# Moving one 64-column subtraction from VectorE to GpSimd in the start-up of a fused attention and MLP kernel

## The chip, the cores and the metric

One core of a Trainium2 chip. The metric is the time of one execution in device microseconds (us). Each run on record has a state, fast or slow, judged from its time and its granted TensorE clock; all runs told of here are fast, with a clock of 0.998 to 1.000.

## The reference

Clustered attention, 4 batches, 8 heads, 768 positions, 64 dimensions: q, k and the 16 centroids of a head are normalised, each q and k row is assigned to the nearest centroid, and attention runs only between rows of equal assignment. The result (3072 x 512) goes through an MLP with exact GELU.

```python
q_assign = np.argmax(np.einsum('bhsd,hcd->bhsc', q_n, c_n), axis=-1)
k_assign = np.argmax(np.einsum('bhsd,hcd->bhsc', k_n, c_n), axis=-1)
mask = q_assign[:, :, :, None] == k_assign[:, :, None, :]
scores = np.where(mask, scale * np.matmul(q, k.transpose(0, 1, 3, 2)), -1000000000.0)
# softmax over the last axis, times v; then gelu(x @ w_in) @ w_out
```

## The kernel before

The kernel computes in fp16. Where fp16 is too coarse for an argmax, a value is kept as two halves: a high part (the cast to fp16) and a low part (the value less the high part). This is done for q and k of every head and once for the centroids, before the first head. A table gives the order of all operations; each engine runs its own in that order (VectorE's in the profile of the kernel before begin so: `cn` 4.85 us, `lok0` 5.27, `chi` 5.75, `clo` 6.00, `loq0` 6.74), and a name with an engine behind it (`hiq0@POOL`) is put there. POOL is GpSimd, DVE is VectorE, ACT is ScalarE, PE is TensorE. The table's part that matters:

```python
TABLE = (
    "loadq0 zero3 ident cent dm ones ssq zero2 root hiq0@POOL loadk0 hik0 eps rnorm "
    "loadk2 loadk1 cn lok0 exptab chi hik1 warm256 ... warm128 trk0 loadq1 clo ctr "
    "cc loq0 trq0 hiq1 loadk3 loadv5 evk0 warm256 ... asnk0 evq0@DVE warm256 ... asnq0 "
    "lok1 hik2 ... trk1 lok2 ... loq1@DVE trq1 amax0 ge0 ... ohtr0 ... sc0a2 ...")   # cut
```

`hik0` is the high part of head 0's k and `lok0` its low part, `trk0` the transposes of both on TensorE, `evk0` the copy of the transposes out of PSUM. `chi` and `clo` are the centroids' high and low parts, `ctr` their two transposes, `cc` the copy of these to `c_cat`, `asnk0` the assignment matmuls, `sc0a2` the first scores. `warm` is a filler matmul that nobody reads. The three operations in question:

```python
c6 = add("DVE", 0.17, -75, lambda: nc.vector.tensor_copy(
    cent_hl[:, 0], cent_n.to_broadcast([H * C, 2, D])), [c5], name="chi")
c7 = add("DVE", 0.22, -74, lambda: nc.vector.tensor_sub(
    cent_hl[:, 1, 0], cent_n[:, 0], cent_hl[:, 0, 0]), [c6], name="clo")
...                                                  # cut
def lo(eng, w=w):                                    # lok0, loq0 on DVE; lok1, lok2 on POOL
    t = T[w + "st", i]
    engine[eng].tensor_sub(t[:, :, D:2 * D], T[w + "raw", i], t[:, :, 0:D])
```

The softmax here doesn't subtract the row's maximum and nothing guards it: scores larger than these inputs give would overflow.

## Time and profile before

| | before |
|---|---|
| median of the first 3 runs | 291.01 us (290.45 to 291.35) |
| span in the profile | 289.3 us, TensorE busy 283.1 |
| q's transposes of head 0 begin | 7.34 us |
| first score matmul begins | 11.89 us |

In a line of the timeline the first number is the start, the second the duration (both us), then engine, source line, operation, output<-inputs and shape; the bracket gives the idle time before it and what ended it. In the lines of waits the numbers are the total, the count and the longest. One more view of the kernel before is ScalarE's timeline: the casts of head 0's and head 1's k.

```profile
4.73 0.51 ACT L381 CAST st<-k_raw 128x384 f16<-128x384 f32 x1 [1.78 <-DMA k_raw<-in_k_dram]
5.15 0.20 ACT L427 ACTIVATE tab<-dm 128x1 f32<-128x1 f16 x1
5.25 0.49 ACT L381 CAST st<-k_raw 128x384 f16<-128x384 f32 x1
```

GpSimd's subtraction for head 1 follows the second cast by 0.08 us; VectorE's for head 0 follows the first.

### The profile page before, as it was taken

To read this page: it belongs to the slowest core of one execution; us is meant where nothing else is said; L and a number is where in the kernel's file an instruction comes from. 1 tells how busy PE (TensorE), PEld (TensorE's weight loads), DVE (VectorE), ACT (ScalarE), POOL (GpSimd) and SP (SyncE) were. 2 spreads that over 40 slices of the span, in tenths; PEclk is the share of its full clock that TensorE was granted. 3 is DMA by queue.
4 is the path that set the end of the run, shared out by engine and by line. 5 is a ranking of instruction groups with operands and counts; after the bars stand their busy time and mean duration, and the time that the engine had idled before them with its cause. 6 is when DMAs were issued, how large, how long until landed. Compare 5 with 4: busy or idle time off the path is not lost.

```text
span 289.3 us, 8384 instructions
## 1 busy us (share of the span) xinstructions
PE 283.1 (98%) x3411; PEld 213.3 (74%) x3411; DVE 206.9 (72%) x501; ACT 232.4 (80%) x323; POOL 108.7 (38%) x151
## 2 busy tenths in 40 slices
PE   7999999999999999999999999999999999999995
PEld 5888776677687777766688888765687788766884
DVE  4899777788989765354997656536769953798853
ACT  3899998699999999857799898767899888498410
POOL 6889971306011714313302644106430020429410
PEclk9999999999999999999999999999999999999999
DMA  7899999577947979949458988656241243010123
GB/s 254 256 241 254 251 292 238 120 130 164 240 120 152 222 183 172 198 132 206 114 139 184 196 210 148 130 159 112 56 97 51 54 103 84 0 57 0 39 76 124
DMA packets 78039, 43.11 MB, mean 149 GB/s; under 512 B 55473, under 2 KB 78001, under 8 KB 78001
## 3 DMA queue, kind: packets, MB, share of 16 engines
q1 hardware_dynamic: 73056, 37.76, 56.7%
q0 software_dynamic: 4224, 4.19, 9.0%
q10 hardware_dynamic: 720, 0.62, 0.6%
q8 instruction: 26, 0.43, 0.6%
q14 instruction: 13, 0.10, 0.1%
HBM read 27.30 MB, written 6.29 MB: 116 GB/s over the span
## 4 chain that ended last, share of the span: by engine, by line
PE 59%; DMA 2%; POOL 1%; DVE 0%; issue 0%; DVEq 0%
PE op L1235 20%; PE hp L919 14%; PE sc_ps L784 11%; PE fx_ps L1055 6%; PE x_ps L816 6%; DMA kqT<-st 2%; PE asn_ps L616 1%; POOL st L519 0%; DVE c L1281 0%; POOL c L1295 0%; POOL st L383 0%; PE fin_ps L887 0%; DVEq L1281 0%
## 5 line engine op out<-in xcount | busy, mean ns | idle before, releaser
L793 ACT ACTIVATE p_sb<-sc_ps 128x768 f16<-128x768 f32 x192 | 146.3, 811 | 9.3 <-PE sc_ps L784 6.8
L784 PE MATMUL sc_ps<-kqT 80*128 80x384 f16 x384 | 93.2, 325 | 0.1
L919 PE MATMUL hp<-xt,w_in_sb 128*128 128x384 f16 x384 | 64.8, 326 | 0.0
L816 PEld LDWEIGHTS <-p_sb 128*128 128x128 f16 x1152 | 47.9, 97 | 10.6 <-issue 0.5
L1235 PEld LDWEIGHTS <-g 128*128 128x128 f16 x480 | 45.5, 97 | 12.2
L919 PEld LDWEIGHTS <-w_in_sb 128*128 128x128 f16 x384 | 36.7, 98 | 23.3
L932 ACT ACTIVATE g<-hp 128x768 f16<-128x768 f32 x48 | 38.9, 811 | 16.6 <-PE hp L919 16.0
L816 PE MATMUL x_ps<-vaug,p_sb 128*128 128x65 f16 x1152 | 52.3, 193 | 0.0
L1235 PE MATMUL op<-w_out_sb,g 128*128 128x256 f16 x288 | 40.1, 272 | 0.0
L784 PEld LDWEIGHTS <-kqT 80*128 80x128 f16 x384 | 31.5, 98 | 3.5 <-issue 0.3
L519 POOL TENSOR_TENSOR st<-k_raw,st 128x384 f16<-128x384 f32 x21 | 19.8, 943 | 28.7 <-DVE st L383 15.7
L1235 PE MATMUL op<-w_st,g 128*128 128x256 f16 x192 | 27.0, 272 | 0.0
L519 POOL TENSOR_TENSOR st<-q_raw,st 128x384 f16<-128x384 f32 x20 | 18.5, 923 | 11.7 <-DVE st L383 6.0
L1235 PEld LDWEIGHTS <-S 128*128 128x128 f16 x192 | 18.1, 97 | 5.2 <-issue 0.3
L632 DVE TENSOR_REDUCE asb<-asn_ps 128x192 f32<-128x384 f32 x24 | 13.3, 553 | 9.3 <-PE asn_ps L616 9.2
L843 DVE TENSOR_TENSOR x_tok<-x_ps,rec 128x384 f16<-128x384 f32 (+1 forms) x40 | 19.0, 476 | 1.1
L383 POOL CAST st<-k_raw 128x384 f16<-128x384 f32 x17 | 9.2, 546 | 25.7 <-DMA kqT<-st 16.4
L836 DVE RECIPROCAL rec<-x_ps 128x6 f32<-128x6 f32 (+1 forms) x40 | 7.5, 187 | 15.5 <-PE x_ps L816 14.8
L383 POOL CAST st<-q_raw 128x384 f16<-128x384 f32 x19 | 10.1, 532 | 15.7 <-DMA q_raw<-in_q_dram 10.0
L383 POOL CAST vaug<-v_raw 128x384 f16<-128x384 f32 x17 | 8.6, 511 | 17.1 <-DMA v_raw<-in_v_dram 11.1
L383 DVE COPY p<-op 128x256 f32<-128x256 f32 x19 | 8.0, 422 | 9.0 <-PE op L1235 8.8
L1235 PE MATMUL op<-w_out_sb,S 128*128 128x256 f16 x96 | 13.8, 272 | 0.1
(120 smaller groups left out, 412.5 us busy)
## 6 DMA issues: line engine op xcount, KB each, us to landing
q_raw<-in_q_dram SPq DMA_DIRECT2D x32, 192.0 KB, 4.1
v_raw<-in_v_dram SPq DMA_DIRECT2D x32, 192.0 KB, 3.9
k_raw<-in_k_dram SPq DMA_DIRECT2D x31, 192.0 KB, 4.0
out_dram<-c SPq DMA_DIRECT2D x45, 128.0 KB, 2.5
w_in_sb<-in_moe_w_in_dram POOLq DMA_DIRECT2D x4, 512.0 KB, 8.5
w_out_sb<-in_moe_w_out_dram POOLq DMA_DIRECT2D x4, 512.0 KB, 10.1
out_dram<-c ACTq DMA_DIRECT2D x3, 128.0 KB, 1.8
kqT<-st SPq DMA_TRANSPOSE x22, 4.0
```

What stands on the lines that cost most here:

```text
L383: engine[eng].tensor_copy(o, i)
L519: engine[eng].tensor_sub(t[:, :, D:2 * D], T[w + "raw", i], t[:, :, 0:D])
L632: nc.vector.tensor_reduce(out=T["asb", i], in_=T["asn", i].rearrange("p n w (a c) -> p n w c a", a=2), axis=AX.X, op=ALU.add)
L784: nc.tensor.matmul(s_ps[:, e, 0:QB], T["kT", i][0:D + C, c * 128:(c + 1) * 128], T["qT", i][0:D + C, t * QB:(t + 1) * QB], start=True, sto ...
L793: nc.scalar.activation(T["p", i, t][:, 2 * cp:2 * cp + 2, :], T["sc", i, t, cp][:, :, 0:QB], ACT_FN.Exp, bias=0.0, scale=float(scale))
L816: nc.tensor.matmul(o, T["p", i, t][:, ch, jj * 128:(jj + 1) * 128], vaugs[turn("va", i)][:, ch, 0:D + 1], start=(ch == 0), stop=(ch == N - 1))
L836: nc.vector.reciprocal(T["rec", key], T["x", key][:, :, D:D + 1])
L843: nc.vector.tensor_tensor(T["xtok", b][:, h // 2, j0:j0 + nn, h % 2 * D:(h % 2 + 1) * D], T["x", key][:, :, 0:D], T["rec", key].to_broadca ...
L919: nc.tensor.matmul(T["hp", hb, fp][:, e, 0:QB], w_in_sb[:, m, f * 128:(f + 1) * 128], T["xt", b][:, m, t * QB:(t + 1) * QB], start=(m == 0 ...
L932: nc.scalar.activation(T["g", hb][:, :, fp, :], T["hp", hb, fp][:, :, 0:QB], ACT_FN.Gelu, bias=0.0, scale=1.0)
L1055: nc.tensor.matmul(o, a[p](m), r[p](m), start=start and m == 0, stop=m == 1, skip_group_check=not start)
L1235: nc.tensor.matmul(T["op", b, key], a()[:, f, j * 128:(j + 1) * 128], w[:, f, :], start=(start and f == 0), stop=(f == NB - 1), skip_group ...
```

## The change

The low part of the centroids goes to GpSimd, in front of GpSimd's subtraction for head 1's k. Its intent is to free VectorE for head 0's q, and to have the low part ready earlier. Besides the table's line breaks the diff is:

```diff
-    "... trk0 loadq1 clo ctr "
+    "... trk0 loadq1 clo@POOL "
+    "ctr ..."
-    c7 = add("DVE", 0.22, -74, lambda: nc.vector.tensor_sub(
-        cent_hl[:, 1, 0], cent_n[:, 0], cent_hl[:, 0, 0]), [c6], name="clo")
+    c7 = add("DVE", 0.22, -74, lambda eng: engine[eng].tensor_sub(
+        cent_hl[:, 1, 0], cent_n[:, 0], cent_hl[:, 0, 0]), [c6], alt={"POOL": 0.3}, name="clo")
```

## The prediction

> **What bounds the kernel now.** I read the shares by engine first, then the stretches of time, then who waited for whom on TensorE, then the instructions of the first 13 us in order of time. The page gives the frame:
>
> ```profile
> span 289.3 us, 8384 instructions
> PE 283.1 (98%) x3411; PEld 213.3 (74%) x3411; DVE 206.9 (72%) x501; ACT 232.4 (80%) x323; POOL 108.7 (38%) x151
> ```
>
> TensorE has work for 283.1 of 289.3 us, so at most 6.2 us are idle on it. A change to one 64-element VectorE instruction can only matter where that idle time lies. The busy time by stretches (columns: stretch, its length, then busy us of PE, PEld, DVE, ACT, POOL) says where:
>
> ```profile
> 5.00:7.30 2.30, 1.64 (x15) 1.04 (x13) 2.10 (x6) 0.83 (x4) 0.91 (x1) 1.00 1.05 361
> 7.30:9.00 1.70, 1.66 (x40) 1.63 (x41) 1.48 (x3) 1.70 (x5) 0.51 (x1) 1.00 0.90 266
> 9.00:12.00 3.00, 3.00 (x63) 2.75 (x61) 2.44 (x7) 1.94 (x4) 3.00 (x4) 1.00 0.84 286
> ...
> 100.00:150.00 50.00, 49.53 (x565) 35.51 (x564) 32.73 (x76) 41.58 (x54) 13.60 (x17) 1.00 0.83 165
> ```
>
> About 1.4 us of the idle time is before the first warm-up matmul, 3.3 us in the last 9.3 us, 0.7 us between 5 and 7.3 us, and 0.5 us near 116 us. From 7.3 us on TensorE is nearly solid, though until 12 us part of that is warm-up filler (matmuls into a tile nobody reads, placed at fixed points of the program order). TensorE's waits name the gap at 7 us:
>
> ```profile
> PE chl_ps L451 <- DVE cent_hl L443: 0.5, 1, 0.5
> PE asn_ps L616 <- DMA kqT<-st: 0.5, 1, 0.5
> PE tr_ps L574 <- DVE st L519: 0.2, 1, 0.2
> ```
>
> The first of these is the instruction that the change moves: TensorE stood 0.5 us before the transpose of the centroids' low part. The third follows at once: another 0.2 us for the low part of head 0's q. In order of time (start, duration, then the instruction):
>
> ```profile
> 5.27 0.56 DVE L519 TENSOR_TENSOR st<-k_raw,st 128x384 f16<-128x384 f32 x1 [0.17 <-ACT st L381]
> 5.75 0.22 DVE L441 CAST cent_hl<-cent_n 128x128 f16<-128x128 f32 x1
> 6.00 0.82 DVE L443 TENSOR_TENSOR cent_hl<-cent_n,cent_hl 128x64 f16<-128x64 f32 x1
> 6.74 0.55 DVE L519 TENSOR_TENSOR st<-q_raw,st 128x384 f16<-128x384 f32 x1
> 7.21 1.24 DVE L383 COPY kqT<-tr_ps 128x768 f16<-128x768 f16 x2
> 8.36 0.55 DVE L519 TENSOR_TENSOR st<-q_raw,st 128x384 f16<-128x384 f32 x1
> ...
> 5.82 0.91 POOL L519 TENSOR_TENSOR st<-k_raw,st 128x384 f16<-128x384 f32 x1 [0.94 <-ACT st L381]
> 8.49 1.19 POOL L519 TENSOR_TENSOR st<-k_raw,st 128x384 f16<-128x384 f32 x1 [1.75 <-DVE kqT L383]
> ```
>
> The 64-element subtraction took 0.82 us, although 384 elements of the same kind take 0.55. It started at 6.00, inside GpSimd's subtraction for head 1's k (5.82 to 6.73), and ended 0.09 us after it. So it was not slow, it was held. It held two things: the q subtraction behind it on VectorE, and the transpose on TensorE, whose later instructions all stand behind it.
>
> [...]above VectorE is held at 6.00; at 8.49 GpSimd's subtraction, begun after VectorE's at 8.36, took 1.19 us instead of its usual 0.91, that is 0.28 more, so it was let go at about 8.77, 0.41 us after VectorE's began.[...] here the trace is used, which has 0.91 us for 384 elements and 1.64 for 768: 1.9 ns an element and 0.18 us fixed[...].
>
> **The change part by part.** Against the kernel before, the order of instructions is the same on TensorE, ScalarE and the DMA queue. VectorE loses the subtraction between the cast of the centroids and the q subtraction of head 0; GpSimd gets it between the cast of q for head 0 and the k subtraction of head 1.
>
> Removed from VectorE: 0.82 us[...]. The q subtraction needs only the load and GpSimd's cast of q (done at 4.88), so it starts behind the cast of the centroids, at 5.90 to 6.00, not 6.74, and ends near 6.5, not 7.29: 0.8 us earlier.
>
> Added to GpSimd: one instruction of 64 elements, 0.18 + 64 x 1.9 ns = 0.30 us. It waits for the cast that ends at 5.97; with the 0.08 us that GpSimd needed after ScalarE's cast at 5.74, it is ready at 6.05. By then VectorE's q subtraction, which waits for nothing at that point, has most likely begun and [...] until 0.41 us after its start, 6.31 to 6.41. So the moved instruction is held too, but for 0.3 us[...], and ends at about 6.6 to 6.7 (its record should read some 0.6 us from 6.05). Before, it ended at 6.82. This part gains only 0.1 to 0.2 us.
>
> TensorE: the transpose of the low part came 0.15 us after its input (6.82, 6.97), so now at about 6.8. The transposes of q stand right behind it; they waited until 7.34 for the q subtraction. Now that is done at 6.5, so they start at about 6.85 to 6.9: 0.45 us earlier. This is the sum that matters. Not 0.8, because the centroid transpose stands in between in TensorE's order.
>
> What follows keeps that step. The copy of head 0's k out of PSUM can start at about 6.5 instead of 7.2, that of q about 0.45 earlier (it needs TensorE's transposes). The c_cat copy on ScalarE, 7.22 to 7.59, comes 0.1 to 0.2 earlier, which is enough, since the assignment matmuls started only at 8.07, behind filler. Filler, k assignments, filler, q assignments, maximum and one-hot of head 0 are a chain in order, each behind the last with gaps under 0.2 us; all shift by about 0.4. The first score matmul (11.89) should come near 11.45.
>
> GpSimd's k subtraction of head 1 moves from 5.82 to about 6.65 and ends near 7.55. Its reader, the transposes at 8.96 (8.5 after the shift), has a us to spare, and GpSimd was idle for 1.75 us before 8.49. It costs nothing.
>
> **The rivals.**[...] If VectorE's q subtraction were late (after 6.05), GpSimd's instruction would run first, 6.05 to 6.35, and the q subtraction from 6.3 to 6.8; q's transposes at 6.9: nearly the same sum. The outcome is robust to who wins, which speaks for a gain at this point of 0.4 to 0.5.
>
> Second: the gain is given back later. The loads wait for raw buffers that GpSimd frees (the queue waited 15.1 us for GpSimd's subtractions before 40 us), ScalarE is 99% busy between 20 and 30 us, and the DMA engines' shares there are above 1. If a transfer paced by the program's start, not by the computation, ended a wait later, a shift of 0.4 us would vanish in it. Against: TensorE shows no named wait between 12 us and the 0.5 us at 116 us; and that one hangs on a transposing DMA whose inputs GpSimd made at 109, behind buffers that earlier computation freed. So most should carry to the end. I give this rival one chance in four of eating more than half: 290.9.
>
> Third: GpSimd's extra instruction delays a later GpSimd chain, which is 98% busy from 20 to 30 us. Its delay, though, falls in the idle stretch before 8.49, and what starts at 8.49 is itself released by work that comes earlier now. If it went wrong it would cost at most the added 0.30 us: 291.3. One in ten.
>
> **Range and chances.** 291.01 less 0.45 at the first head, times about 0.85 for what is lost on the way, is 290.6. The three runs before spread over 0.9 us (290.45 to 291.35), more than the effect, so the range is wider than the argument: 290.0 to 291.3 for 8 in 10. A gain of 2% would be 5.8 us and the whole 5 to 9 us stretch is 4 us long; a loss of 2% has no source in 0.30 us of added work. So 0.5% for faster, 99% for within 2%, 0.5% for slower.
>
> **What would show it right or wrong.** Right: the q subtraction on VectorE begins before 6.1 and takes 0.55; the moved subtraction stands on GpSimd from about 6.05 with some 0.6 us; the waits of TensorE for it shrink from 0.5 to about 0.35, and the 0.2 us wait for q vanishes; q's transposes begin at 6.8 to 7.0, the first score matmul near 11.45, and the span is 0.3 to 0.5 shorter. Wrong: the moved instruction takes more than 0.8 us or ends later than 6.82, so that TensorE waits longer; q's transposes are early but the first score matmul stays at 11.9 (a wait in head 0's chain that I missed); or both are early and a new wait on TensorE after 12 us takes it back.

The sum: q's subtraction moves from 6.74 to between 5.90 and 6.00 (0.8 us), q's transposes from 7.34 to between 6.85 and 6.9 (0.45 us), and 291.01 less 0.45 times 0.85 comes to 290.6. GpSimd's rate is the trace's: 0.91 us for its subtraction of 384 elements (L519), 1.64 us for its two-input operation of 768 (L949). For what VectorE holds, the figure is the one measured at 8.36: GpSimd's instruction is held until 0.41 us after the start of VectorE's.

## The result and the profile after

In the first measurement the changed kernel has a median of 290.39 us (289.75 to 290.72, 4 runs) against 290.88 (290.45 to 291.35, 4 runs). The ratio is 0.998, with a 95% interval of 0.9956 to 1.0005. A ratio is the mean time of one kernel's fast runs over that of the other's of the same rounds, so it is not quite the ratio of the medians. It is "the same" at 2%, and by itself not even clear of zero.

The page of the changed kernel:

```profile
span 288.0 us, 8383 instructions
PE 282.2 (98%) x3411; PEld 212.9 (74%) x3411; DVE 206.5 (72%) x500; ACT 232.4 (81%) x323; POOL 110.0 (38%) x152
```

VectorE has one instruction less, GpSimd one more. The timeline of VectorE and GpSimd in the start-up:

```profile
5.35 0.56 DVE L519 TENSOR_TENSOR st<-k_raw,st 128x384 f16<-128x384 f32 x1 [0.25 <-ACT st L381]
5.83 0.22 DVE L441 CAST cent_hl<-cent_n 128x128 f16<-128x128 f32 x1
5.97 0.55 DVE L519 TENSOR_TENSOR st<-q_raw,st 128x384 f16<-128x384 f32 x1
6.52 0.56 DVE L383 COPY kqT<-tr_ps 128x768 f16<-128x768 f16 x1
...
6.13 0.55 POOL L443 TENSOR_TENSOR cent_hl<-cent_n,cent_hl 128x64 f16<-128x64 f32 x1 [1.25 <-DVE cent_hl L441]
6.64 0.91 POOL L519 TENSOR_TENSOR st<-k_raw,st 128x384 f16<-128x384 f32 x1
```

The q subtraction starts right behind the cast (5.97, before 6.74). The moved one is held by it and ends at 6.68 (before 6.82). TensorE's timeline from the low part's transpose on, and its waits:

```profile
6.74 0.23 PE L451 MATMUL chl_ps<-ident,cent_hl 128*128 128x128 f16 x1 [0.20 <-POOL cent_hl L443]
6.80 0.50 PE L574 MATMUL tr_ps<-ident,st 128*128 128x128 f16 x6
...
11.34 0.49 PE L784 MATMUL sc_ps<-kqT 80*128 80x384 f16 x2
```

```profile
PE tr_ps L574 <- DVE st L519: 0.7, 1, 0.7
PE chl_ps L451 <- POOL cent_hl L443: 0.2, 1, 0.2
```

The wait for the low part fell from 0.5 to 0.2 us and that for q is gone. The 0.7 us is for head 0's k and not from the change: its transposes began at 5.97 and before at 5.89, but the fillers ahead of them had ended earlier in this execution. q's transposes came 0.54 us earlier, the first scores 0.55 earlier (11.34, before 11.89). Head 0's k was subtracted 0.08 us later here (5.35, before 5.27); counted from there q's transposes came 0.62 us earlier (1.45 us behind it, before 2.07).

The spans differ by 1.3 us, more than 0.55. TensorE's wait of 0.5 us near 116 us, which the prediction shows, is absent here. The experiments say whether that belongs to the change.

### The profile page after: what moved, and what is told of

Same layout as the page of the kernel before. It is cut to its first block, busy times and chain, and to the rows that moved or that the text cites. A ratio compares the mean times of both kernels' runs of the same rounds, so it can differ in the third digit from the quotient of the medians.

```text
span 288.0 us, 8383 instructions
## 1 busy us (share of the span) xinstructions
PE 282.2 (98%) x3411; PEld 212.9 (74%) x3411; DVE 206.5 (72%) x500; ACT 232.4 (81%) x323; POOL 110.0 (38%) x152
## 4 chain that ended last, share of the span: by engine, by line
PE 94%; ACT 2%; DMA 1%; issue 1%; POOL 1%; DVE 0%; ACTq 0%; POOLq 0%
PE op L1235 26%; PE hp L919 22%; PE sc_ps L784 21%; PE x_ps L816 12%; PE fx_ps L1055 6%; PE asn_ps L616 2%; ACT p_sb L793 2%; PE tr_ps L574 2%; DMA cent_sb<-in_centroids_dram 1%; PE asn_ps L613 1%; PE asn_ps L614 1%; PE warm_ps L373 1%; PE fin_ps L887 1%; PE oh_ps L692 1%; PE trs_ps L574 0%
## 5 line engine op out<-in xcount | busy, mean ns | idle before, releaser
L519 POOL TENSOR_TENSOR st<-k_raw,st 128x384 f16<-128x384 f32 x21 | 19.8, 945 | 26.6 <-DVE st L383 15.7
L519 POOL TENSOR_TENSOR st<-q_raw,st 128x384 f16<-128x384 f32 x20 | 18.5, 926 | 7.0 <-DVE st L383 5.3
L949 POOL TENSOR_TENSOR S<-S,g 128x768 f16<-128x768 f16 x5 | 8.2, 1643 | 15.0 <-PE fx_ps L1055 6.4
```

The lines of the kernel that those rows point to most:

```text
L949: engine[eng].tensor_sub(o, a, c)
```

## The experiments

Two theories went in. **H**: GpSimd's subtraction for head 1's k held VectorE's low part; the change ends the hold, q's transposes gain some 0.5 us, and the gain is carried to the end. **L**: it is lost on the way. Others (V, I, J, R) arose from single runs and are named in the texts. All 12 runs gave correct results. The first four ran on one chip beside 11 runs of the kernel before (median 290.55, mean 290.44). The other eight ran on a second chip beside 11 (the last four: the same and one more, 12; median 290.71, mean 290.71).

| run | median (mean) us | ratio, 95% interval | q's transposes | first scores | span of the profile |
|---|---|---|---|---|---|
| before, first profile | 290.88 (290.89) | | 7.34 | 11.89 | 289.3 |
| changed, first profile | 290.39 (290.32) | 0.998 (0.9956-1.0005) | 6.80 | 11.34 | 288.0 |
| e1 changed again | 290.39 (290.40) | 1.0000 (0.9981-1.0019) | 6.57 | 11.11 | 288.5 |
| e2 low part behind head 1's k | 291.11 (291.03) | 1.0022 (1.0002-1.0041) | 7.67 | 12.20 | 289.4 |
| e3 head 1's k on VectorE | 290.92 (290.86) | 1.0016 (0.9993-1.0039) | 6.81 | 12.23 | 289.0 |
| e4 high part earlier | 290.42 (290.43) | 1.0001 (0.9982-1.0020) | 7.17 | 11.72 | 289.0 |
| e5 before, k load first | 290.50 (290.38) | 0.9987 (0.9964-1.0011) | 6.56 | 11.11 | 288.4 |
| e6 changed, k load first | 290.47 (290.42) | 0.9989 (0.9965-1.0012) | 6.83 | 11.42 | 288.8 |
| e7 both e4 and e6 | 290.02 (290.06) | 0.9972 (0.9948-0.9995) | 6.69 | 11.24 | 289.0 |
| e8 changed, 20 fillers more | 292.72 (292.62) | 1.0065 (1.0045-1.0085) | 9.06 | 13.59 | 291.2 |
| e9 before, with a fence | 290.11 (290.15) | 0.9981 (0.9957-1.0004) | 6.61 | 11.16 | 288.3 |
| e10 changed again | 290.16 (290.13) | 0.9979 (0.9957-1.0001) | 6.63 | 11.17 | 288.4 |
| e11 low part twice | 290.63 (290.56) | 0.9994 (0.9974-1.0014) | 6.90 | 11.43 | 288.5 |
| e12 as e7, again | 290.50 (290.39) | 0.9988 (0.9967-1.0008) | 6.86 | 11.40 | 288.6 |

The means are worked out from the single runs. The next-to-last two columns are starts in the run's one profile.

### e1: the changed kernel again

No edit.

> The changed kernel once more, with five rounds. Theory H (hold removed, 0.5 us gained at head 0's q transposes, carried to the end): ratio to the kernel before 0.9975 to 0.9990, with q's transposes at 6.7 to 6.9 us and the first score matmul near 11.35. Rival L (the early gain is lost on the way, the first measured 0.5 us was luck): ratio 0.999 to 1.001 though the early times repeat. The TensorE wait of 0.5 us near 116 us, which the first profile of the change lacks, may or may not be there; if it comes and goes between runs of the same kernel it is not an effect of the change.

q's transposes began at 6.57, the first scores at 11.11, earlier still than in the first profile. Yet the times agree with the kernel before: means of 290.40 and 290.44. This looks like L. But the runs before spread from 289.42 to 291.31 and those of the changed kernel only from 290.19 to 290.67, so in this call more seems to vary without the change; that is not shown, since in e10's call the changed kernel spreads over 1.04 us too. And the wait near 116 us is back in this profile, at 0.4 us (and in e10's again). So it comes and goes, and the 0.75 us by which the first pair of spans differs beyond the start-up is no effect of the change: from the first scores to the end this profile takes 277.4 us, as long as the kernel before.

### e2: the low part behind head 1's k

```diff
-    "... trk0 loadq1 clo@POOL ctr cc ... asnq0 lok1 ..."
+    "... trk0 loadq1 lok1 clo@POOL ctr cc ... asnq0 ..."
```

> The moved subtraction still on GpSimd, but behind head 1's k subtraction instead of ahead of it; TensorE, VectorE and ScalarE orders as in the changed kernel. Theory H: what counts is when the low part is ready, so it comes at 6.7 to 7.1 plus 0.3, its transpose at 7.1 to 7.4, q's transposes right behind, and the time goes back to that of the kernel before (ratio 0.999 to 1.002). Rival V (it helps because VectorE is rid of the instruction): VectorE's copy of k is as early as in the changed kernel (6.5) and the ratio stays near 0.998.

VectorE's timeline, then GpSimd's:

```profile
6.10 1.27 DVE L519 TENSOR_TENSOR st<-q_raw,st 128x384 f16<-128x384 f32 x1
...
6.05 0.91 POOL L519 TENSOR_TENSOR st<-k_raw,st 128x384 f16<-128x384 f32 x1 [1.17 <-ACT st L381]
6.92 0.62 POOL L443 TENSOR_TENSOR cent_hl<-cent_n,cent_hl 128x64 f16<-128x64 f32 x1
```

A cascade of holds. GpSimd's k subtraction, 0.05 us ahead, holds VectorE's q subtraction (1.27 instead of 0.55), and this holds the low part (0.62, unheld 0.31 in e4). q's transposes come at 7.67, later than before. The kernel is 0.63 us slower in the mean than the changed kernel of the same call (291.03, 290.40). VectorE is as free of the instruction as in the changed kernel, so V's forecast (0.998) failed; but VectorE was held in another way, which V's forecast of an early copy did not allow for. What this shows is that the place of the instruction on GpSimd decides, not the engine alone.

### e3: head 1's k taken off GpSimd

```diff
-    "... asnq0 lok1 hik2 ..."          # on the kernel before
+    "... asnq0 lok1@DVE hik2 ..."
```

> The kernel before, with the low part on VectorE as it was, but head 1's k subtraction taken off GpSimd and put on VectorE behind the copies of head 0. GpSimd then reads nothing while the low part is computed. Theory H[...]: the low part takes 0.22 to 0.25 us instead of 0.82, q's subtraction ends near 6.7, q's transposes start near 6.8. Rival I (the instruction is slow in itself, by its mixed types or by waiting for the cast before it): still 0.8 us. The whole time: VectorE has 0.55 us more ahead of head 0's maximum, which should eat some 0.3 of the 0.5 us, so a ratio of 0.998 to 1.001, of little weight.

VectorE's timeline:

```profile
6.06 0.23 DVE L443 TENSOR_TENSOR cent_hl<-cent_n,cent_hl 128x64 f16<-128x64 f32 x1
...
8.29 1.27 DVE L519 TENSOR_TENSOR st<-q_raw,st 128x384 f16<-128x384 f32 x1
```

This answers rival I. The same instruction on the same engine takes 0.23 us with GpSimd idle (here from 4.98 to 8.11), 0.82 beside GpSimd's subtraction (before). The expected 0.22 to 0.25 us is also what VectorE's cast of the centroids and their scaling take in the profile before (0.22, 0.25). q's transposes came at 6.81, as in the changed kernel. Then head 1's q subtraction ran into GpSimd's next one, took 1.27 us, and the first scores slid to 12.23, 0.9 us later than in the changed kernel's first profile, where I had expected some 0.3. The hold was moved, not removed.

### e4: the centroids' high part earlier

```diff
-    "loadk2 loadk1 cn lok0 exptab chi hik1 ..."
+    "loadk2 loadk1 cn chi lok0 exptab hik1 ..."
```

> The changed kernel with the centroids' high part (the cast) put ahead of head 0's k subtraction on VectorE, into the 0.2 us that VectorE is idle there. Theory H: the cast ends near 5.35 and not 6.05, the low part on GpSimd ends at 6.0 to 6.1 (held by k's subtraction until about 5.75), so q's transposes wait for q's subtraction alone and start at 6.4 to 6.55, 0.3 us earlier than in the changed kernel; ratio to the kernel before 0.9965 to 0.998. Rival L: early times move, the whole does not.

ScalarE's, GpSimd's and VectorE's timelines:

```profile
5.55 0.51 ACT L381 CAST st<-k_raw 128x384 f16<-128x384 f32 x1 [2.59 <-DMA k_raw<-in_k_dram]
...
5.46 0.31 POOL L443 TENSOR_TENSOR cent_hl<-cent_n,cent_hl 128x64 f16<-128x64 f32 x1 [0.56 <-DVE cent_hl L441]
...
6.09 0.56 DVE L519 TENSOR_TENSOR st<-k_raw,st 128x384 f16<-128x384 f32 x1 [0.71 <-ACT st L381]
```

The low part was unheld here and took 0.31 us (the prediction's estimate was 0.30), ending at 5.77. It gained nothing in this execution, because head 0's k landed late: cast at 5.55, against 4.54 in e1 with the same loads in the same order. q's transposes waited for k, at 7.17. The mean time is that of the changed kernel; whether k landed late in the other five runs too is not known, so why they gained nothing is not shown. My expectation failed on something I had not looked at: when this load lands.

### e5, e6, e7: head 0's k load first

e5 is the kernel before, e6 the changed kernel, e7 the changed kernel with e4's edit, each with head 0's two loads exchanged between the queues:

```diff
-    "loadq0 zero3 ident cent dm ... hiq0@POOL loadk0 hik0 ..."
+    "loadk0 zero3 ident cent loadq0 dm ... hiq0@POOL hik0 ..."
-            eng = "SP" if i or name != "k" else "ACT"
+            eng = "SP" if i or name != "q" else "ACT"
```

> The kernel before, with head 0's k load put first on the sync queue and its q load second on ScalarE's queue (they were the other way round). In the profiles so far head 0's k was cast between 4.54 and 5.55 us, and everything behind it moved with it. Theory J (the spread between runs, as large as the effect of the change, comes from the landing of this load): k is cast by 4.1 to 4.5, the low part is still held on VectorE[...] when head 1's k is ready first, the spread of its runs shrinks below 1 us, and its time is 0.2 to 0.6 us under that of the kernel before. Rival: the landing does not matter for the whole, ratio 1.000.

> The changed kernel with the same exchange of head 0's loads. With theory H and J together the change is then measured without the jitter: 0.3 to 0.6 us under the run before it (ratio of the two times 0.998 to 0.999), q's transposes at 6.4 to 6.6. Rival L: the same time as the run before it within 0.1 us.

> Both: the exchange of head 0's loads and the centroids' high part ahead of head 0's k subtraction, on the changed kernel. Theory H: the low part is ready by 6.0, q's transposes start at 6.3 to 6.45, and the time is 0.1 to 0.3 us under the run with the exchange alone; 0.5 to 1 us under the kernel before. Rival L: the early instructions move, the whole does not.

In all three profiles head 0's k was now cast at 3.42. VectorE's and GpSimd's timelines of e5:

```profile
5.81 0.23 DVE L443 TENSOR_TENSOR cent_hl<-cent_n,cent_hl 128x64 f16<-128x64 f32 x1
...
6.07 1.21 POOL L519 TENSOR_TENSOR st<-k_raw,st 128x384 f16<-128x384 f32 x1 [0.97 <-ACT st L381]
```

and of e6:

```profile
5.06 0.86 DVE L519 TENSOR_TENSOR st<-k_raw,st 128x384 f16<-128x384 f32 x1
...
4.99 0.52 POOL L383 CAST st<-q_raw 128x384 f16<-128x384 f32 x1 [0.52 <-DMA q_raw<-in_q_dram]
```

e5 is the turning point. It has the low part on VectorE, exactly as before, and it is not held: VectorE came first (5.81), GpSimd second (6.07), and now GpSimd paid (1.21 us, held by VectorE's q subtraction, which had begun at 5.95). q's transposes began at 6.56, without the change and earlier than with it in e6. So the hold does not come with the instruction order alone: it is the outcome of a race that depends on when loads land. In e6 the late q load made GpSimd's cast of q hold VectorE's k subtraction (0.86 us): a new hold. The runs of e5 and e6 show no difference: means 290.38 and 290.42, with some 0.8 us either way left open by their scatter. The forecasts of q's transposes at 6.4 to 6.6 and of 0.3 to 0.6 us between the two failed: in these profiles e5 had no hold left to remove, and e6 had the new one.

J's forecast for the time of e5 came out in the mean (0.38 us under the kernel before, whose 11 runs have a mean of 290.76), though not clear of zero. The spread did not shrink as J had it: e5 ran from 289.62 to 291.04, e6 from 289.56 to 291.44. So the landing of head 0's k moves the start-up, but it is not the main source of the spread of the whole. e7's starts missed their forecast: its low part ended at 6.22, not by 6.0, and q's transposes began at 6.69, not 6.3 to 6.45. Its time seemed the best of all, 0.9972; see e12.

### e8: how much of a shift arrives

```diff
-    "... cc loq0 trq0 ..."            # on the changed kernel
+    "... cc loq0 warm256 (20 times) trq0 ..."
```

> The changed kernel with 20 more filler matmuls of 256 columns in front of head 0's q transposes, some 2.1 us on TensorE[...]. It measures how much of a shift at this place arrives at the end. If a shift is carried whole (theory H): 2.0 to 2.2 us longer than the changed kernel, about 292.5. Rival L (later work is paced by transfers, not by this chain): under 1 us longer, below 291.4.

In the changed kernel's profile five take 0.55 us (at 7.14), so 20 some 2.2 us, an estimate.

TensorE's timeline (the source lines are shifted by two by the longer table):

```profile
6.88 2.35 PE L375 MATMUL warm_ps<-dm 128*128 128x256 f16 x20
9.06 0.50 PE L576 MATMUL tr_ps<-ident,st 128*128 128x128 f16 x6
```

q's transposes were put off from 6.88 to 9.06, 2.18 us. The time is 2.49 us more than that of the changed kernel on the same chip (e10: 290.13; 292.62). The shift arrives whole at the end, against L. The 0.3 us above 2.18 is within what the means leave open. This is a delay; that work moved earlier also arrives is read from the 14 profiles further below.

### e9: the hold taken away without moving the work

On the kernel before, a one-column copy on GpSimd that reads the low part, ahead of its k subtraction. In GpSimd's order the subtraction stands behind it, so it should not start before the low part is done.

```diff
+    fence = const.tile([H * C, 1], FP16, name="fence")
+    add("POOL", 0.1, -73, lambda: nc.gpsimd.tensor_copy(fence, cent_hl[:, 1, 0, 0:1]), [c7],
+        name="fence")
-    "... loadq1 clo ctr ..."
+    "... loadq1 clo fence ctr ..."
```

> The kernel before, with the low part left on VectorE, and one GpSimd copy of a single column that reads the low part, put ahead of head 1's k subtraction. GpSimd runs in order, so its subtraction can no longer begin before the low part is done: the hold is gone without moving the work. Theory R (what the change removes is a race: head 1's k, if its load lands early enough,[...] as in the profile of before; in other runs it comes later and nothing is held): low part 0.23 us, q's transposes at 6.6 to 6.9, the time within 0.3 us of the changed kernel's in this call, and both under the kernel before by 0.2 to 0.6 us. Rival V (VectorE must be rid of the instruction): the changed kernel is faster than this one by over 0.3 us.

VectorE's, then GpSimd's timeline:

```profile
5.86 0.23 DVE L443 TENSOR_TENSOR cent_hl<-cent_n,cent_hl 128x64 f16<-128x64 f32 x1
...
6.15 0.45 POOL L446 COPY fence<-cent_hl 128x1 f16<-128x1 f16 x1 [1.24 <-DVE cent_hl L443]
6.56 0.91 POOL L522 TENSOR_TENSOR st<-k_raw,st 128x384 f16<-128x384 f32 x1
```

The words cut from R say what GpSimd gains when head 1's k lands early; in the profile before its subtraction began ahead of VectorE's low part (5.82, 6.00). GpSimd kept its order: the cast of head 1's k ended at 6.14, yet the subtraction began at 6.56, behind the fence (6.15 to 6.60).

Low part 0.23 us, q's transposes 6.61, mean 290.15: the same as the changed kernel in the same call (6.63, 290.13). So nothing here says that VectorE must be rid of the instruction, though the scatter of six runs each leaves some 0.5 us either way open, more than the 0.3 us of rival V. It fits that an order between the two instructions that does not depend on a load is enough. One reservation: in this profiled execution head 1's k was cast at 5.63, so GpSimd would have come second without the fence too. The fence's effect on a held execution was not caught in a profile.

### e10: the changed kernel beside them

> The changed kernel again, beside the others of this call. Theory R: 0.2 to 0.5 us under the kernel before, since only some of the runs before are held (five of seven starts of this program order profiled so far, going by when head 0's and head 1's k were cast); a ratio of 0.9983 to 0.9993, whose interval may well take in 1. Theory H without the race: 0.5 us, 0.9983.

0.9979, 0.58 us below the kernel before in the mean, a little more than expected and still with 1 just inside the interval.

### e11: the low part twice

```diff
-    c7 = add(..., lambda eng: engine[eng].tensor_sub(...), ...)
+    c7 = add(..., lambda eng: [engine[eng].tensor_sub(...) for _ in range(2)], ...)
```

> The changed kernel with the moved subtraction done twice in a row on GpSimd. It measures the instruction by itself: the first is held by VectorE's q subtraction (0.55 us), the second meets no reader of SBUF on VectorE (a copy from PSUM), so it should take 0.31 us, as in the one run where nothing held it. Theory H: q's transposes 0.3 to 0.35 us later than in the changed kernel, and the time 0.2 to 0.4 us longer. Rival L: no longer.

GpSimd's, then TensorE's timeline:

```profile
5.84 0.93 POOL L443 TENSOR_TENSOR cent_hl<-cent_n,cent_hl 128x64 f16<-128x64 f32 x2 [0.94 <-DVE cent_hl L441]
...
6.83 0.23 PE L451 MATMUL chl_ps<-ident,cent_hl 128*128 128x128 f16 x1 [0.53 <-POOL cent_hl L443]
```

Two take 0.93 us, one held takes 0.55: the second costs 0.38, not 0.31. VectorE's copy from PSUM lay beside it (6.28 to 6.84). Such a copy did not hold GpSimd's longer subtraction in the first profile of the changed kernel: the copy took 0.56 us (at 6.52), the subtraction 0.91 (at 6.64), each its usual time. Why the second took 0.07 us more is not shown. TensorE's wait for it grew from 0.20 (e10) to 0.53, by 0.33, and the mean time by 0.43 (290.56, 290.13; from the scatter of the runs some 0.0 to 0.9). The low part's end does set q's transposes here, and it fits that what it loses is lost in the whole.

### e12: e7 again

> The changed kernel with head 0's loads exchanged and the centroids' high part ahead, once more: the first time it was 0.9972 of the kernel before (0.9948 to 0.9995). If that was no luck: 0.9965 to 0.9985 again, and under the changed kernel of this call by 0.1 to 0.5 us.

It was luck, as far as this repeat tells: 0.9988 and 0.26 us above the changed kernel of the same call in the mean. VectorE's and GpSimd's timelines show why the exchange of loads is no clear gain:

```profile
4.89 0.60 DVE L439 TENSOR_SCALAR cent_n<-cent_sb,cent_rnorm 128x64 f32<-128x64 f32 x1
...
4.94 0.50 POOL L383 CAST st<-q_raw 128x384 f16<-128x384 f32 x1 [0.47 <-DMA q_raw<-in_q_dram]
```

GpSimd's cast of q, 0.5 us later than with q's load first, falls on the scaling of the centroids, which took 0.60 us instead of 0.25; in e7 it fell on the cast behind it (0.41 instead of 0.22). So a VectorE cast or scaling was lengthened here too, not only a subtraction; by the recorded starts the scaling was 0.05 us ahead (4.89, 4.94), so who held whom there is inferred from the durations. No version was found that beats the changed kernel beyond doubt; the fence of e9 equals it in the mean.

## Why the prediction was right, point by point

- **The hold.** Right, and shown by the clean reversal: the instruction takes 0.82 us beside GpSimd's subtraction begun 0.18 us earlier, 0.23 when GpSimd is idle (e3) or begins only after its end (e5: 6.04, 6.07; e9: 6.09, 6.15). So 0.59 us of the 0.82 was hold. What the two instructions contend for is not shown.
- **The order after the change.** Right: the q subtraction began at 5.97 (said 5.90 to 6.00), the moved instruction ran 6.13 to 6.68 (said 6.05 to some 6.65), head 1's k subtraction began at 6.64 (said 6.65).
- **The sum, 0.45 us at q's transposes.** Measured 0.54 in the first pair: 6.80 where 6.85 to 6.9 was said. The difference is in the step from the low part's end to its transpose, taken as 0.15 us from the profile before and 0.06 after (6.68, 6.74). TensorE's wait for the low part was 0.2 us, where about 0.35 was said. First scores 11.34, said 11.45.
- **The factor for what is carried, 0.85.** Not borne out: no loss on the way shows. e8 carries its delay of 2.18 us whole, and over the 14 profiles the span less the start of the first scores is 276.7 to 277.8 us, while that start moves from 11.11 to 13.59. That holds for early starts as for late ones: its mean is 277.2 us for the nine profiles that start before 11.5 and for the five that start later. So the later chain was not paced from the program's start.
- **The time, 290.6 us in 290.0 to 291.3.** 290.39, inside; but the range was so wide that the kernel before, at 290.88 in the same measurement, lies inside it too. The difference of the means in the three comparisons was 0.58, 0.04 and 0.58 us, on average 0.40, where 0.4 was predicted; from the scatter of the single runs I work out some 0.1 to 0.7 for that average. No comparison alone excludes zero.
- **What was missed.** The prediction took one profile as the kernel. Whether the low part is held depends on which comes first, VectorE's low part (in the order of the kernel before 0.73 us behind the start of head 0's k subtraction) or GpSimd's subtraction (0.57 us behind the start of head 1's k cast). With these two offsets the ten profiles that keep the loads' order read:

  | profile | head 0's k subtraction begins | low part would begin on VectorE | head 1's k cast begins | GpSimd would begin | first |
  |---|---|---|---|---|---|
  | before | 5.27 | 6.00 | 5.25 | 5.82 | GpSimd |
  | changed | 5.35 | 6.08 | 5.62 | 6.19 | VectorE |
  | e1 (changed) | 5.13 | 5.86 | 5.66 | 6.23 | VectorE |
  | e2 | 5.49 | 6.22 | 5.47 | 6.04 | GpSimd |
  | e3 | 5.33 | 6.06 | 5.41 | 5.98 | GpSimd |
  | e4 | 6.09 | 6.82 | 6.07 | 6.64 | GpSimd |
  | e8 | 5.43 | 6.16 | 5.41 | 5.98 | GpSimd |
  | e9 | 5.13 | 5.86 | 5.63 | 6.20 | VectorE |
  | e10 (changed) | 5.18 | 5.91 | 5.16 | 5.73 | GpSimd |
  | e11 | 5.07 | 5.80 | 5.47 | 6.04 | VectorE |

  GpSimd would come first in six and second in four, and the three executions of the changed kernel itself already differ. What a hold costs is read from head 0's k subtraction to q's transposes: 2.07 us with the low part held (before), 1.47 and 1.48 with it unheld on VectorE (e5; e3 and e9), 1.44 to 1.45 in the three profiles of the changed kernel. So the change gains 0.6 us in a held start and next to nothing in another, and 0.6 us in six of ten starts is some 0.4 us on average, an estimate from those rows. That fits 0.40, and fits that a comparison can show nothing; that e1's comparison did so for this reason is not shown, since only one execution of the kernel before itself was profiled.
- **Luck in the number.** The prediction came to its gain of 0.4 us as 0.45 us in every execution times 0.85 for loss on the way. By the estimate above it is some 0.6 us in about six of ten executions, with nothing lost on the way. The two products agree by luck; the mechanism of a held start was right, how often it occurs was not foreseen.
- **The rivals.** GpSimd winning against VectorE's q subtraction was never seen in the changed order. The gain given back later: against it stand e8 and the constant time behind the first scores. A delayed GpSimd chain: not seen; its subtraction for head 2 began at 8.28, before at 8.49.
- **What the prediction would have read wrongly.** It named a span shorter by 0.3 to 0.5. The first pair gave 1.3, and much of the rest was the wait near 116 us, which is also in two of the changed kernel's three profiles. Judged by that pair alone the change would look about three times as good as the means say.

Left open: what makes the runs of one kernel spread over up to 2 us. Head 0's k landing alone is not it (e5, e6).

## What to carry to other kernels

When a short VectorE instruction takes several times what it takes alone (here 0.82 us, alone 0.23), look at GpSimd's line at the same time before moving anything; then fix the order of the two instructions, by moving one or by a dependence (e9, not yet seen to act on a held start), so that it does not hang on which load lands first. A wait that one profile shows may be a race: compare the starts of its two sides in several executions before counting its length as a gain. Where TensorE is busy to the end and a shift is carried whole, as in e8, a start-up gain is worth its own length, and no more.

## What the profiles show of the hold, the load and the small instruction

- How long a hold lasts. VectorE's hold ended before its record did: in the kernel before, GpSimd's subtraction begun 0.13 us after VectorE's of 0.55 us lost only 0.28 us (1.19, usually 0.91), so it was let go 0.41 us after VectorE's start. In the changed kernel the moved instruction ended at 6.68; less its 0.31 us it was let go at 6.37, 0.40 us after VectorE's start at 5.97. The two unheld durations on VectorE (0.23 us for 64 elements, 0.55 for 384) give 1.0 ns an element, so some 0.38 us for 384 elements without the fixed part, an estimate near the length of the hold. The other way round the hold lasted to about the end of GpSimd's record: a held VectorE subtraction of 384 elements ended 0.41 us after it in e2 (6.96, 7.37) and in e6 (5.51, 5.92).
- Who is held. In these pairs the instruction whose record begins first kept its usual time and the other was held. GpSimd first: before (5.82, 0.91 us; VectorE 6.00, 0.82 instead of 0.23), e2 (6.05, 0.91; 6.10, 1.27 instead of 0.55) and e6 (4.99, 0.52; 5.06, 0.86 instead of 0.55). VectorE first: before (8.36, 0.55; GpSimd 8.49, 1.19 instead of 0.91), e4 (6.57, 0.55; 6.64, 1.26) and e5 (5.95, 0.55; 6.07, 1.21). The scaling in e12, slow though recorded 0.05 us ahead, stays open. Going by when the two sides of the race were ready, GpSimd would come first in one of three executions of the changed kernel, and in six of the ten profiles.
- The landing of one load at the start varies between executions: head 0's k was cast at 4.52 to 5.55 us in ten profiles with the same order of loads.
- GpSimd's subtraction of 64 elements took 0.31 us unheld (e4), and a second one right behind a first added 0.38 us (e11).
